# The first twelve attention steps of a fused attention + gated MLP kernel, written in another order: a split first group, two score tiles, and PE transposes for batch 0

## The chip, the cores and the metric

One core of a Trainium2 chip runs the whole kernel in one launch. The metric is device time in microseconds (us), the median of several executions. One execution was also profiled. PE is the matrix engine, DVE the vector engine, ACT the scalar engine (exponentials, logarithms, activations), POOL the general engine, and SP issues DMAs. PE writes to PSUM, a small memory of eight banks; a tile of 512 float32 per partition is one bank.

## The reference

Eight batches, twelve heads, 448 positions, head size 64. Attention with normalised q and k comes first, then a gated MLP over the concatenated heads.

```python
def rmsnorm(x, g):
    return x / np.sqrt(np.mean(x * x, axis=-1, keepdims=True) + 1e-06) * g
q_n, k_n = rmsnorm(q, g_q), rmsnorm(k, g_k)
attn = softmax(q_n @ k_n.T / np.sqrt(64))        # sums + 1e-9
x = (attn @ v) with the heads side by side       # (8, 448, 768)
h = np.maximum(x @ w_in, 0.0)                    # (8, 448, 1024)
u, v = h[..., :512], h[..., 512:]
v_n = (v - mean(v)) / np.sqrt(var(v) + 1e-06)
v_s = einsum('ts,bsd->btd', w_spatial, v_n) + b_spatial[None, :, None]
out = (u * v_s) @ w_out                          # (8, 448, 768) float32
```

## The kernel before

Positions are laid out 112 to a partition set, four chunks of them (NC). Four heads make a **group**, three groups a batch, so there are 24 groups, and four **steps** a group: step t computes scores and exponentials for two heads and two chunks of keys of group G = t // 4. There are 96 steps (0 to 95) and three more turns of the loop that only finish what is behind. Every engine takes its instructions strictly in the order in which the code is written (`manual_schedule`), so the order of the calls in the loop is the schedule.

**Preparing a group.** `load` brings q and k of a group (float32) on SP's queue into a ring of four tiles each (`qf`, `kf`). `squares` multiplies each by itself into `sqt` (POOL; ACT or DVE where `eng` says so), `reduce` sums them (DVE), `rstd` makes 1/rms on ACT (`lnms`, `rs`), and `scaled` multiplies the raw tile with it into bf16 (`n`). The products must then be transposed so that the head dimension lies on the partitions. Group 0 uses PE (`transposes`), and DVE brings the result from PSUM; every other group uses `transpose_dma`, a DMA on SP's queue (`qT`, `kr`), and `k_scale` multiplies k by the gains (`kT`) on DVE.

**A step.** `scores` writes four products of 448 columns into one tile `pss` of four PSUM banks, `expo` takes the exponential on ACT into `et`. In the first twelve steps each step goes in two halves of two banks, in the others in one piece. One group later `sums` and `recip` make the softmax denominators, and `values` (twice) and `xt_store` (DVE) the attention output `xt`. The other four PSUM banks (`ps_w`) rotate among everything else.

**The MLP** of batch b starts at step 12 b + 15: `unit_v`, `stats`, `ln_rstd`, `ln_apply`, `unit_u`, `unit_s`, `unit_o`, spread over twelve steps. `unit_v` and `unit_u` need `w_in`, which POOL's queue loads at step 1; `w_sp`, `w_out` and `bst` follow at step 4. At step 15 DVE copies `bst` into `w_spT`, and `w_sp_unit` transposes one quarter of `w_sp` in each of steps 15 to 18. The v tiles of a batch (`load_v`) and all weights are issued on POOL's queue, behind POOL's own arithmetic.

Of the kernel before, what the change touches and what calls it, by code (L numbers as in the profile page):

```python
# [18 lines left out]
def kernel(  # L19
# [34 lines left out]
    v_pool = ctx.enter_context(tc.tile_pool(name="vp", bufs=3))  # L54
# [3 lines left out]
    m_pool = ctx.enter_context(tc.tile_pool(name="mp", bufs=2))  # L58
    o_pool = ctx.enter_context(tc.tile_pool(name="op", bufs=4))
# [6 lines left out]
    def load(G, i, l0=0, nl=4):  # L66
        b, g = divmod(G, NG)
        if (G, i) not in raw:
            raw[G, i] = qk_pool.tile([P, 4, NC * D], FP, name="qf" if i == 0 else "kf")
        sync.dma_start(out=raw[G, i][:, l0:l0 + nl], in_=(q_g, k_g)[i][b][g][:, l0:l0 + nl])  # L70
# [30 lines left out]
    w_in = const.tile([128, 6, DF], BF)  # L101
# [73 lines left out]
    def qk_tiles(G):
        if G not in qkt:
            qkt[G] = (qt_pool.tile([128, NC, 2, P], BF, name="qT"),
                      qt_pool.tile([128, NC, 2, P], BF, name="kT"))
        return qkt[G]
# [374 lines left out]
```

## Time and profile before

| what | value |
| --- | --- |
| median of 3 runs | 356.57 us (354.12 to 356.83) |
| profiled execution, its own time | 354.63 us |
| its span from first to last instruction | 352.8 us |
| busy in the span: PE, ACT, DVE, POOL | 82%, 63%, 60%, 53% |

The profiled execution has its own time, 1.83 us more than its span; rows of the trace add up to the span. The busy shares are means over two different stretches: the first 80 us, in which PE is busy 33.39 us, and the rest. So the shares above bound nothing by themselves.

### The profile page before, as it was taken

Reading aid. Unit: us, or ns where it says so; the run is one execution under the profiler, and the core shown is the slowest. Engines: PE = TensorE matmul, PEld = TensorE weight load, DVE = VectorE, ACT = ScalarE, POOL = GpSimd, SP = SyncE. Lnnn points to the kernel's source line nnn. Section 1 sums busy time; section 2 is a strip of 40 time slices with the busy share of each in tenths; the row PEclk is TensorE's granted clock in tenths of the full one; section 3 lists DMA queues with packets and bytes.
Section 4 is the critical chain, followed back from the end, with each engine's and each line's share of the span. In section 5 each row is a group of like instructions: output and inputs, shape, how many; then the busy total and the mean of one; then the engine's idle time right before and its main releaser. Section 6 shows DMA issues by size and latency. Waiting matters only on the chain.

```text
span 352.8 us, 5856 instructions
## 1 busy us (share of the span) xinstructions
PE 288.7 (82%) x2338; PEld 134.5 (38%) x2338; DVE 210.6 (60%) x352; ACT 222.0 (63%) x273; POOL 186.3 (53%) x113
## 2 busy tenths in 40 slices
PE   0222634688999989997999989998999899999993
PEld 0111201224435433542344434443444345445552
DVE  3385304226887587757764886488648865745551
ACT  2334434375778768874876786778677867785331
POOL 7259850926746774687197549654965484000000
PEclk9999999999999999998999999999999999999998
DMA  7979999497346994899339983999299554302305
GB/s 194 245 159 167 203 187 203 89 148 156 55 110 144 209 243 106 145 213 248 101 82 215 242 170 69 220 252 166 58 223 261 62 54 111 99 2 62 96 0 158
DMA packets 81651, 52.26 MB, mean 148 GB/s; under 512 B 44271, under 2 KB 77264, under 8 KB 81624
## 3 DMA queue, kind: packets, MB, share of 16 engines
q1 hardware_dynamic: 69216, 43.59, 57.2%
q0 software_dynamic: 12400, 8.30, 16.6%
q8 instruction: 18, 0.29, 0.4%
q14 instruction: 9, 0.07, 0.1%
q10 hardware_dynamic: 8, 0.00, 0.0%
HBM read 38.58 MB, written 11.01 MB: 141 GB/s over the span
## 4 chain that ended last, share of the span: by engine, by line
issue 37%; POOL 34%; PE 18%; DMA 7%; ACT 1%; DVE 1%; ACTq 0%; POOLq 0%; DVEq 0%
POOL sqt L148 19%; POOL n L168 12%; PE ps L336 5%; DMA qT<-n 4%; PE ps L283 4%; PE ps L312 3%; PE pss L217 2%; PE ps L257 2%; PE ps L322 2%; POOL vt L74 2%; ACT et L228 1%; DMA out_dram<-osb 1%; DMA g_row<-in_g_k_dram 1%; PE ps L238 1%; POOL w_in L121 1%
## 5 line engine op out<-in xcount | busy, mean ns | idle before, releaser
L228 ACT ACTIVATE et<-pss 112x1792 bf16<-112x1792 f32 (+1 forms) x109 | 160.4, 1483 | 68.8 <-PE pss L217 67.9
L168 POOL TENSOR_TENSOR n<-qf,rs 112x1024 bf16<-112x1024 f32 (+1 forms) x25 | 48.5, 1939 | 111.3 <-ACT rs L163 109.4
L217 PE MATMUL pss<-qT,kT 64*112 64x448 bf16 x384 | 64.6, 408 | 39.9 <-ACT et L228 33.0
L155 DVE TENSOR_REDUCE ms<-sqt 112x16 f32<-112x1024 f32 (+1 forms) x50 | 58.1, 1171 | 40.4 <-POOL sqt L148 38.4
L265 DVE TENSOR_TENSOR xt<-ps,rc 128x448 bf16<-128x448 f32 x48 | 29.6, 617 | 41.2 <-PE ps L257 35.7
L217 PEld LDWEIGHTS <-kT 64*112 64x112 bf16 x384 | 22.1, 134 | 79.2 <-issue 66.8
L257 PE MATMUL ps<-et,vt 112*32 112x448 bf16 x768 | 49.6, 382 | 0.0
L336 PE MATMUL ps<-w_out,gt 128*112 128x384 bf16 x256 | 47.5, 330 | 1.7 <-DVE osb L341 1.4
L283 PE MATMUL ps<-w_in,xt 128*112 128x512 bf16 x192 | 45.8, 383 | 0.1
L148 POOL TENSOR_TENSOR sqt<-qf 112x1024 f32<-112x1024 f32 x23 | 44.4, 1932 | 0.0
L312 PE MATMUL ps<-xt,w_in 128*128 128x448 bf16 x192 | 41.3, 361 | 2.2 <-DVE vs L275 2.2
L168 POOL TENSOR_TENSOR n<-kf,rs 112x1024 bf16<-112x1024 f32 x21 | 40.0, 1906 | 0.0
L148 POOL TENSOR_TENSOR sqt<-kf 112x1024 f32<-112x1024 f32 x21 | 39.7, 1890 | 0.0
L336 PEld LDWEIGHTS <-gt 128*112 128x112 bf16 x256 | 31.3, 129 | 18.4 <-issue 11.1
L283 PEld LDWEIGHTS <-xt 128*112 128x112 bf16 x192 | 23.4, 130 | 19.4 <-issue 6.6
L341 DVE COPY osb<-ps 112x384 f32<-112x384 f32 x46 | 24.4, 553 | 7.5 <-PE ps L336 5.9
L322 PE MATMUL ps<-w_spT,vn 112*128 112x448 bf16 (+1 forms) x128 | 26.9, 353 | 0.0
L257 PEld LDWEIGHTS <-vt 112*32 112x32 bf16 x768 | 16.8, 100 | 26.4 <-issue 19.5
L312 PEld LDWEIGHTS <-w_in 128*128 128x128 bf16 x192 | 17.6, 100 | 24.2 <-issue 11.1
L238 PE MATMUL ps<-et,ones 112*32 112x448 bf16 x384 | 24.8, 382 | 0.0
L325 DVE TENSOR_TENSOR gt<-ps,us 128x448 bf16<-128x448 f32 x32 | 20.0, 625 | 6.8 <-PE ps L322 4.5
L289 DVE BATCH_NORM_STATS2 s<-vs 112x6 f32<-112x512 bf16 x32 | 21.8, 680 | 2.5 <-ACT vs L273 2.5
(47 smaller groups left out, 184.0 us busy)
## 6 DMA issues: line engine op xcount, KB each, us to landing
out_dram<-osb SPq DMA_DIRECT2D x31, 336.0 KB, 3.6
qf<-in_q_dram SPq DMA_DIRECT2D x23, 448.0 KB, 6.3
kf<-in_k_dram SPq DMA_DIRECT2D x23, 448.0 KB, 7.4
vt<-in_v_dram POOLq DMA_DIRECT2D x8, 672.0 KB, 13.0
w_in<-in_moe_w_in_dram POOLq DMA_DIRECT2D x4, 384.0 KB, 11.9
w_out<-in_moe_w_out_dram POOLq DMA_DIRECT2D x1, 768.0 KB, 13.7
qf<-in_q_dram SPq DMA_DIRECT2D x2, 224.0 KB, 3.6
kf<-in_k_dram SPq DMA_DIRECT2D x2, 224.0 KB, 3.8
```

The source lines that it names most:

```text
L148: (eng or pool).tensor_tensor(out=t[:, 0:nl, :], in0=x, in1=x, op=ALU.mult)
L155: dve.tensor_reduce(out=sqs[G][:, i, NC * l0:NC * (l0 + nl)], in_=sqt.pop((G, i, l0))[:, 0:nl, :].rearrange("p l (c d) -> p (l c) d", d=D) ...
L168: (eng or pool).tensor_tensor(out=nrm[G, i][:, :, l0:l0 + nl, :].rearrange("p c l d -> p l c d"), in0=raw[G, i][:, l0:l0 + nl, :].rearrang ...
L217: pe.matmul(out=pss[:, 2 * c + h, 0:S], lhsT=kT[64 * h:64 * h + 64, c0 + c, pr, :], rhs=qT[64 * h:64 * h + 64, :, pr, :], start=True, stop ...
L228: act.activation(out=exps[G, pr][:, 2 * c0 + a:2 * c0 + a + m, :], in_=pss[:, a:a + m, 0:S], func=AF.Exp, bias=0.0, scale=1.0)
L238: pe.matmul(out=ps[32 * l:32 * l + 32, 0:S], lhsT=ones, rhs=exps[G, l // 2][:, 2 * c + l % 2, :], start=(c == 0), stop=(c == NC - 1), tile ...
L257: pe.matmul(out=ps[32 * l:32 * l + 32, 0:S], lhsT=vb[b][:, 3 * l + g, c, 32 * half:32 * half + 32], rhs=exps[G, l // 2][:, 2 * c + l % 2, ...
L265: dve.tensor_tensor(out=xts[b][:, 2 * g + half, :], in0=pst.pop((G, half))[:, 0:S], in1=rec[G], op=ALU.mult)
L283: pe.matmul(out=ps[0:P, :], lhsT=xts[b][:, j, c * P:(c + 1) * P], rhs=w_in[:, j, DH:DF], start=(j == 0), stop=(j == 5))
L312: pe.matmul(out=ps[:, 0:S], lhsT=w_in[:, j, 128 * f:128 * f + 128], rhs=xts[b][:, j, :], start=(j == 0), stop=(j == 5))
L322: pe.matmul(out=ps[:, 0:S], lhsT=vn_t[b % 2][0:kp, c, 128 * f:128 * f + 128], rhs=w_spT[0:kp, c, :, :].rearrange("p c s -> p (c s)"), star ...
L336: pe.matmul(out=ps[0:P, 0:384], lhsT=gts[b][:, f, c * P:(c + 1) * P], rhs=w_out[:, f, r], start=(f == 0), stop=(f == 3))
```

## The change

The part of the program ahead of step 16 is written anew; the work from there on is the same, with smaller rings of buffers.

- Group 0 is split in two halves with tiles of their own (`first`), and ACT takes three of its four squares ahead of everything else. q and k of groups 0 to 4 are issued on SP before anything waits (`f`, `qf`, `kf`).
- For the first twelve steps, `pss` becomes two tiles `pse` of two banks each (`scores_half`, `expo_half`). At step 12 that pool is closed and `pss` takes its banks.
- Groups 1 to 4 are transposed on PE and brought from PSUM by DVE (`qe`, `ke`); `transpose_dma` starts with group 5. Of groups 1 to 4 the products `scaled` are shared by POOL and DVE.
- PE does 50 matmuls of 128 columns on the identity at the start, and eight in each of steps 0 to 3 (`dummies`); nothing reads them.
- `load_v(0)` moves behind the first work on POOL; `w_in` is two tensors loaded by four DMAs each, at steps 5 and 9; `w_sp` goes to step 9, `w_out` and `bst` to step 12.
- The rings `vp`, `mp` and `op` go from 3, 2 and 4 buffers to 2, 1 and 3. For later groups `k_scale` moves two steps later.

```diff
+    ps_e = early_pools.enter_context(tc.tile_pool(name="ps_e", bufs=2, space=PSUM, side="right"))
...
-    v_pool = ctx.enter_context(tc.tile_pool(name="vp", bufs=3))
+    v_pool = ctx.enter_context(tc.tile_pool(name="vp", bufs=2))
...
-    m_pool = ctx.enter_context(tc.tile_pool(name="mp", bufs=2))
-    o_pool = ctx.enter_context(tc.tile_pool(name="op", bufs=4))
+    m_pool = ctx.enter_context(tc.tile_pool(name="mp", bufs=1))
+    o_pool = ctx.enter_context(tc.tile_pool(name="op", bufs=3))
...
-    for G in (1, 2):
+    for G in (1, 2, 3):
         load(G, 0)
         load(G, 1)
...
+    def dummies(n):
+        for _ in range(n):
+            pe.matmul(out=ps_d[:, 0:128], lhsT=ident, rhs=ident, start=True, stop=True)
+
+    dummies(50)
...
     def transposes(G, pr):
...
-        qT, kT = qk_tiles(G)
-        dve.tensor_copy(out=qT[:, :, pr, :], in_=ps[:, 0:4, 0:P])
-        dve.tensor_scalar(out=kT[:, :, pr, :], in0=ps[:, 4:8, 0:P], scalar1=g2_col, scalar2=None,
-                          op0=ALU.mult)
+        qT = early_qt.tile([128, NC, P], BF, name=f"qe{pr}")
+        kT = early_qt.tile([128, NC, P], BF, name=f"ke{pr}")
+        dve.tensor_copy(out=qT, in_=ps[:, 0:4, 0:P])
+        dve.tensor_scalar(out=kT, in0=ps[:, 4:8, 0:P], scalar1=g2_col, scalar2=None, op0=ALU.mult)
+        qkt[G, pr] = (qT, kT)
...
+    def scores_half(t, c):
+        sct[t, c] = ps_e.tile([P, 2, 512], FP, name="pse")
+        scores_of(sct[t, c], t, c)
+
+    def expo_half(t, c):
+        expo_of(sct[t, c], t, 2 * c, 2)
...
+    squares(0, 0, 0, 2, act)
+    squares(0, 1, 0, 2, act)
+    squares(0, 0, 2, 2, act)
+    reduce(0, 0, 0, 2)
+    reduce(0, 1, 0, 2)
+    reduce(0, 0, 2, 2)
+    rstd(0, 0, 2)
+    squares(0, 1, 2, 2, act)
+    scaled(0, 0, 0, 2)
+    scaled(0, 1, 0, 2, dve)
...
+    squares(1, 0, eng=act)
+    squares(1, 1)
+    scores_half(0, 0)
+    scores_half(0, 1)
+    transposes(0, 1)
+    load_v(0)
+    squares(2, 0)
...
         if t == 0:
-            rstd(1)
-            scaled(1, 0)
-            scaled(1, 1, eng=dve)
-            squares(2, 0)
+            reduce(1, 0)
+            reduce(1, 1)
+            squares(2, 1)
         elif t == 1:
-            transpose_dma(1, 0)
-            transpose_dma(1, 1)
-            squares(2, 1, eng=dve)
+            rstd(1)
+            scaled(1, 1, eng=dve)
+            scaled(1, 0, eng=dve)
+        elif t == 4:
             reduce(2, 0)
             reduce(2, 1)
-        elif t == 2:
-            k_scale(1)
+        elif t == 5:
             rstd(2)
             scaled(2, 0)
-        elif t == 3:
             scaled(2, 1, eng=dve)
...
+            squares(3, 0)
+            squares(3, 1, eng=dve)
+            load_w_in(1)
...
+        elif t == 12:
+            reduce(4, 0)
+            reduce(4, 1)
+            load_w_out()
+        elif t == 13:
+            rstd(4)
+            scaled(4, 0)
+            scaled(4, 1, eng=dve)
...
+        if t < 4:
+            dummies(8)
...
+        if t == 15:
+            transposes(4, 0)
+            transposes(4, 1)
+        if t < 12:
+            turn = n == 3
+            if turn:
+                transposes(G + 1, 0)
+            if t + 1 < 12:
+                scores_half(t + 1, 0)
+            if turn:
+                transposes(G + 1, 1)
+            if t + 1 < 12:
+                scores_half(t + 1, 1)
+            if t == 7:
+                reduce(3, 0)
+                reduce(3, 1)
+            if t == 8:
+                rstd(3)
```

On POOL, these are the instructions from the product of group 2 (`n_264`) to the products of group 4 in the kernel before. `sqt` is a square, `n` a product with 1/rms, and DMA rows are issues.

```order
L168 TENSOR_TENSOR n_264<-qf,rs 112x4x4x64
L148 TENSOR_TENSOR sqt<-qf 112x1024
L148 TENSOR_TENSOR sqt<-kf 112x1024
L126 DMA w_sp<-in_moe_w_spatial_dram 112x1792
L127 DMA w_out<-in_moe_w_out_dram 128x4x768
L128 DMA bst<-in_moe_b_spatial_dram 17x448
L168 TENSOR_TENSOR n_331<-qf,rs 112x4x4x64
L168 TENSOR_TENSOR n_333<-kf,rs 112x4x4x64
```

On POOL in the changed kernel, this stands from the product of group 3 (`n_570`) to the squares of group 6.

```order
L189 TENSOR_TENSOR n_570<-qf,rs 112x4x4x64
L135 DMA w_in_u<-in_moe_w_in_dram 32x6x512 x4
L167 TENSOR_TENSOR sqt<-qf 112x1024
L80 DMA vt<-in_v_dram 112x12x256
L167 TENSOR_TENSOR sqt<-kf 112x1024
L140 DMA w_sp<-in_moe_w_spatial_dram 112x1792
L143 DMA w_out<-in_moe_w_out_dram 128x4x768
L144 DMA bst<-in_moe_b_spatial_dram 17x448
L189 TENSOR_TENSOR n_714<-qf,rs 112x4x4x64
L167 TENSOR_TENSOR sqt<-qf 112x1024
L167 TENSOR_TENSOR sqt<-kf 112x1024
```

The loads of weights and of the second v tile now stand between the work of groups 3 and 4, and the product of group 4 on POOL (`n_714`) has them all ahead of it.

On DVE, this stands around step 15 in the kernel before: the last `xt` of batch 0, a sum of squares, then the copies for `w_spT`, two relu (`vs`), and the k of group 4 (`kT`).

```order
L265 TENSOR_TENSOR xt<-ps,rc 128x448 x2
L155 TENSOR_REDUCE ms<-sqt 112x16
L471 CAST w_spT<-bst 17x448
L137 COPY w_spT<-ps 112x448
L275 TENSOR_SCALAR vs<-ps 112x512 x2
L155 TENSOR_REDUCE ms<-sqt 112x16
L205 TENSOR_SCALAR kT<-kr,g_col 128x896
```

And this in the changed kernel, from the product of group 4 (`n_716`) to the operands of group 4 (`qe_814`, `ke_815`).

```order
L189 TENSOR_TENSOR n_716<-kf,rs 112x4x4x64
L293 TENSOR_TENSOR xt<-ps,rc 128x448 x2
L173 TENSOR_REDUCE ms<-sqt 112x16 x3
L507 CAST w_spT<-bst 17x448
L153 COPY w_spT<-ps 112x448
L303 TENSOR_SCALAR vs<-ps 112x512 x2
L205 COPY qe_814<-ps 128x448
L206 TENSOR_SCALAR ke_815<-ps,g_col 128x448
```

Three sums (both of group 5, the first of group 6) and the copy of `bst` now stand ahead of the operands that step 16 needs.

## Rows read from the trace of the kernel before

**Rows 1.** Stretch, length, busy us of PE, PEld, DVE, ACT, POOL; PEclk; DMA.

```profile
50.00:60.00 10.00, 3.78 (x24) 1.37 (x25) 3.69 (x5) 3.10 (x5) 0.00 (x0) 1.00 1.28 211
...
90.00:100.00 10.00, 10.00 (x81) 4.31 (x79) 8.47 (x18) 7.91 (x12) 7.46 (x4) 1.00 0.51 102
```

**Rows 2.** Timeline to the first exponential: start us, us, engine, line, [idle before <-releaser].

```profile
7.19 0.31 ACT L162 ACTIVATE lnms<-ms,eps 112x16 f32<-112x16 f32 x1 [2.68 <-DVE ms L155]
...
9.43 0.93 PE L185 MATMUL ps<-ident,n 112*128 112x112 bf16 x8 [3.42 <-POOL n L168]
...
10.70 0.44 DVE L191 TENSOR_SCALAR kT<-ps,g_col 128x448 bf16<-128x448 bf16 x1
...
12.24 0.92 ACT L228 ACTIVATE et<-pss 112x896 bf16<-112x896 f32 x1 [4.49 <-PE pss L217]
```

**Rows 3.** Timeline of ACT: exponentials of steps 4 and 8, half of `recip`.

```profile
34.54 1.72 ACT L228 ACTIVATE et<-pss 112x896 bf16<-112x896 f32 x2 [1.08 <-PE pss L217]
...
39.18 0.58 ACT L247 ACTIVATE rc<-lr 128x448 f32<-128x448 f32 x1
...
55.11 1.72 ACT L228 ACTIVATE et<-pss 112x896 bf16<-112x896 f32 x2 [4.54 <-PE pss L217]
```

**Rows 4.** Timeline: DVE and POOL on groups 1 and 2.

```profile
23.03 1.23 DVE L168 TENSOR_TENSOR n<-kf,rs 112x1024 bf16<-112x1024 f32 x1 [0.65 <-ACT rs L163]
23.08 2.94 POOL L168 TENSOR_TENSOR n<-qf,rs 112x1024 bf16<-112x1024 f32 x1 [4.03 <-ACT rs L163]
24.18 2.92 DVE L148 TENSOR_TENSOR sqt<-kf 112x1024 f32<-112x1024 f32 x1
...
25.98 2.87 POOL L148 TENSOR_TENSOR sqt<-qf 112x1024 f32<-112x1024 f32 x1
```

**Rows 5.** Timeline: the transposing DMAs of group 3 and what waits.

```profile
45.47 7.04 SPq L197 DMA_TRANSPOSE qT<-n  x1
...
53.57 0.45 DVE L205 TENSOR_SCALAR kT<-kr,g_col 128x896 bf16<-128x896 bf16 x1 [9.17 <-DMA kr<-n]
53.94 0.62 DVE L265 TENSOR_TENSOR xt<-ps,rc 128x448 bf16<-128x448 f32 x1
```

**Rows 6.** Timeline of POOL: issues and a square.

```profile
28.80 0.99 POOL L74 DMA_DIRECT2D vt<-in_v_dram  x1
29.77 2.50 POOL L121 DMA_DIRECT2D w_in<-in_moe_w_in_dram  x4
...
34.83 1.88 POOL L148 TENSOR_TENSOR sqt<-qf 112x1024 f32<-112x1024 f32 x1
...
39.10 0.80 POOL L127 DMA_DIRECT2D w_out<-in_moe_w_out_dram  x1
```

**Rows 7.** An issue in the first 90 us: count, KB, us to landing.

```profile
bst<-in_moe_b_spatial_dram POOLq DMA_DIRECT2D x1, 29.8 KB, 13.1
```

**Rows 8.** Timeline around step 16: PE and DVE.

```profile
77.68 1.69 PE L257 MATMUL ps<-et,vt 112*32 112x448 bf16 x16
...
82.96 1.22 DVE L155 TENSOR_REDUCE ms<-sqt 112x16 f32<-112x1024 f32 x1 [2.92 <-POOL sqt L148]
...
83.50 0.59 PE L217 MATMUL pss<-qT,kT 64*112 64x448 bf16 x4
84.02 0.94 PE L238 MATMUL ps<-et,ones 112*32 112x448 bf16 x16
...
84.21 0.99 DVE L471 CAST w_spT<-bst 17x448 bf16<-17x448 f32 x1
...
85.54 1.28 DVE L275 TENSOR_SCALAR vs<-ps 112x512 bf16<-112x512 f32 x2
```

**Rows 9.** Timeline of SP and ACT: an output's first issue, a later copy.

```profile
109.84 0.35 SPq L345 DMA_DIRECT2D out_dram<-osb  x1
...
114.15 0.49 ACT L339 ACTIVATE osb<-ps 112x384 f32<-112x384 f32 x1
```

**Rows 10.** DMA issues of the page, whole span: KB each, us to landing.

```profile
out_dram<-osb SPq DMA_DIRECT2D x31, 336.0 KB, 3.6
```

More of the change, by code (lines that the diff above doesn't have):

```diff
@@ L67, in load @@
         b, g = divmod(G, NG)
[L68 to L70 removed]
+        if nl == 4:
+            t = qk_pool.tile([P, 4, NC * D], FP, name="qf" if i == 0 else "kf")
+        else:
+            t = first.tile([P, 2, NC * D], FP, name=f"f{i}{l0}")
+        raw[G, i, l0] = t
+        sync.dma_start(out=t, in_=(q_g, k_g)[i][b][g][:, l0:l0 + nl])
     def load_v(b):
@@ L98 @@
     make_identity(nc, ident)
-    w_in = const.tile([128, 6, DF], BF)
+    w_in_u = const.tile([128, 6, DH], BF)
+    w_in_v = const.tile([128, 6, DH], BF)
     w_out = const.tile([128, 4, DM], BF)
@@ L165, in scaled @@
+        rst[G, l0] = st_pool.tile([P, 2, 4 * nl], FP, name="rs")
+        act.activation(out=ln, in_=sqs[G, l0], func=AF.Ln, bias=eps[0:P, :], scale=1.0 / D)
+        act.activation(out=rst[G, l0], in_=ln, func=AF.Exp, bias=0.0, scale=-0.5)
     def scaled(G, i, l0=0, nl=4, eng=None):
-        if (G, i) not in nrm:
-            nrm[G, i] = qn_pool.tile([P, NC, 4, D], BF, name=f"n{i}")
+        if nl == 4:
+            t = qn_pool.tile([P, NC, nl, D], BF, name=f"n{i}")
+        else:
+            t = first.tile([P, NC, nl, D], BF, name=f"n{i}{l0}")
@@ L173, in scaled @@
             op=ALU.mult)
[L175 to L179, printed above, removed]
     def transposes(G, pr):
@@ L202 @@
-    krs = {}
+            krs[G] = t
+        else:
+            qts[G] = t
+    krs, qts = {}, {}
     def k_scale(G):
-        dve.tensor_scalar(out=qkt[G][1], in0=krs.pop(G), scalar1=g2_col, scalar2=None, op0=ALU.mult)
+        kT = qt_pool.tile([128, NC, 2, P], BF, name="kT")
+        dve.tensor_scalar(out=kT, in0=krs.pop(G), scalar1=g2_col, scalar2=None, op0=ALU.mult)
+        for pr in range(2):
+            qkt[G, pr] = (qts[G][:, :, pr, :], kT[:, :, pr, :])
     exps, xts = {}, {}
-    pss = ps_sc.tile([P, 4, 512], FP, name="pss")
@@ L232, with step @@
+    def step(t):
+        for c in range(2):
+            scores_of(pss[:, 2 * c:2 * c + 2, :], t, c)
+        expo_of(pss, t, 0, 4)
     rec, pst = {}, {}
@@ L349 @@
     NST = NGT * 4
-    for pr in range(2):
-        l = 2 * pr
-        squares(0, 0, l, 2, act)
-        squares(0, 1, l, 2, dve)
-        reduce(0, 0, l, 2)
-        reduce(0, 1, l, 2)
-        rstd(0, l, 2)
-        if pr == 0:
-            dve.tensor_copy(out=g2_col, in_=ps_g[:, 0:1])
-        scaled(0, 0, l, 2)
-        scaled(0, 1, l, 2, dve)
-        transposes(0, pr)
-        if pr == 0:
-            scores(0, 0)
-            scores(0, 1)
-            expo(0, 0)
-    squares(1, 0)
-    squares(1, 1, eng=dve)
@@ L445 @@
             transpose_dma(T, 1)
-        if n == 0 and 3 <= K < NGT:
-            k_scale(K)
         if moe:
```

169 lines of the change are left out of this document (85 added, 84 removed).

## The prediction

> **What bounds the kernel now.** I read the busy times by stretch first, then the time lines of the slow stretch. From 90 to 100 us PE is busy 10.00 of 10.00 us; from 50 to 60 it is busy 3.78, and POOL not at all [rows 1]. So the kernel is two things: a start in which everything waits for everything, and from step 16 on a PE that never stops. The four score products of step 16 start at 83.50 [rows 8]. The change leaves PE's work from there on as it is, so what it is worth is the time at which these four start. I call it X; before it is 83.50.
>
> What the start waits for is in the time lines. The first exponential is at 12.24 [rows 2], step 4 at 34.54 and step 8 at 55.11 [rows 3], about 5 us a step, while one step's exponentials take 1.72. Step 8 came late because SP held one transposing DMA for 7.04 us behind other traffic, and DVE, next in its queue, sat 9.17 us for the k of that DMA [rows 5].
>
> **The change, part by part.** I follow the new order with durations of before, each instruction behind the one ahead of it on its engine.
>
> *First exponential.* The chain from `rstd` (7.19) to the exponential (12.24) is the same work. ACT takes the k square as well, so `rstd` comes at about 6.8, and the transposes and scores take half their time if PE runs at its upper level (below). I put it at 11.1.
>
> *Group 0.* Eight halves of 0.92 [rows 2] follow with no wait for PE, since there are two tiles. In their middle ACT must do `rstd(1)`, which waits until DVE has done its evictions and two sums (1.22 each [rows 8]), at 15.1: half a us lost, and half a us of work. Group 0 ends at 19.4.
>
> *Group 1.* Both products are on DVE, and POOL squares group 2 beside them. What that costs is in the time line [rows 4]: a product that takes DVE 1.23 ran first, POOL's, begun beside it, took 2.94 and so ended one square's length (1.88 [rows 6]) after it, and DVE's next, a square of about 1.24 alone, took 2.92. Engine by engine they went one after the other. In the new order DVE starts at 15.8 behind a square begun at 14.5; 0.6 of wait, 1.23, 1.88 of POOL, 1.23 make 20.7. Without the mutual wait it would be 18.3. PE's transposes, two evictions of at most 0.44 [rows 2] and the scores (some 1.3 more) give step 4 at 22.9. The old 34.54 is thus 11.6 earlier.
>
> The Trainium skill ("SBUF — State Buffer", "SBUF: two separate sides") says that DVE with two SBUF inputs and a GpSimd instruction exclude each other for whole instructions; the trace agrees (2.94 and 2.92 [rows 4]). The page says the same lock keeps GpSimd from writing descriptors while DVE is in a two-port mode, which speaks against sharing; no row here shows it. As an estimate by that page, each of the two `w_in` issue blocks could lose one DVE instruction of 1.24, and the sum below would be some 1 us later.
>
> *PE's level.* Sixteen `values` products took 1.69 us at 77.68 and sixteen `sums` of equal size 0.94 at 84.02 [rows 8]; the granted clock reads 1.00 in the sparse and in the dense stretch alike [rows 1], so I take the two levels (1.2 and 2.4 GHz) from the durations. PE rose between the two, late and not at the start. At the low level a step costs PE 1.69 and four scores (twice 0.59 [rows 8]), 2.9, more than ACT; at the high level ACT's 1.72 rules. I keep both: group 1 takes 8.6 on ACT (4 x 1.72, two of 0.58 for `recip` [rows 3], some 0.55 for `rstd`, whose first half is 0.31 [rows 2]) or 11.4 on PE.
>
> The Trainium skill ("TensorE: Matmul & The Clock Gate", "HAM oscillation — how this bites in real kernels") says that PE drops to its lower rate when it waits long between bursts. That speaks against the dummies: they stand in steps 0 to 3, and the waits come at the turns of group behind them. By the page the late figure of each pair here would hold; if the dummies' level lasted, the early one. The pair ends 2.9 apart.
>
> *Group 2.* `rstd(2)` at 28.2 or 28.9; then on DVE and POOL in turn 1.23, 1.9, 1.24; DVE must also do two `xt` (0.62 each [rows 5]) before it evicts. Step 8 comes at 35.1 or 36.8, before at 55.11. Two halves, the second operands, `recip` and the sums of group 3 later, `rstd(3)` ends at 40.0 or 41.5.
>
> *The POOL queue.* From here POOL sets the time. It holds, in order: the product of group 3 behind DVE's (1.23 + 1.9), four issues of `w_in` (2.50), a square (1.88), the v issue (0.99), a square (1.88) [rows 6]: 10.4, at 50.4 or 51.9. The issues of `w_sp`, `w_out` and `bst` (at most 0.80 each [rows 6]) fit behind, beside the sum and `rstd(4)`, which ends at 52.3 or, as ACT is behind by then at the low level, 55.2. Then the product of group 4 (3.1 with DVE's ahead) and three squares (5.6): 61.0 or 63.9. On DVE a sum (1.22), the `bst` copy (0.99), a copy of an eviction's size (0.44 [rows 2]), two relu (1.28) and the evictions (0.83) stand between that and the scores of step 16 [rows 8, 2]: X = 65.8 or 68.7. No work hides this chain: PE and ACT have nothing else.
>
> *The weights.* `bst` is issued at 52.4 to 54 and took 13.1 to land before [rows 7]. Again that long, the copy on DVE would start at 65.5 to 67 instead of 62.2 to 65, so 3 us late. Those 13 us were in a queue full of `w_in` and transposes; the new queue holds `w_in`'s second half and a v tile. The cost is between 0 and 3; I take 1, nearer the low end because the transposes are gone. With the middle of the pair, 67.3, X = 68.3: 15.2 earlier.
>
> *Given back later.* Group 5 is the first with a transposing DMA, issued at step 16, and its `k_scale` stands at step 18 ahead of the statistics that ACT waits for; if it lands like an output (3.6 [rows 10]) DVE waits up to 3.7 and ACT up to 2, of which PE's queue hides most. I take 0.5. At the end the fourth output tile must wait for the first one's DMA since `op` has three: 0.4. `vp` and `mp` with fewer buffers cost nothing: v has 14 steps to land, and PE's order keeps a batch's MLP behind the last one's. If the cover of v went, it would hold PE for the rest of its landing.
>
> Sum: 354.63 (the profiled execution's own time, 1.94 below the median of 356.57) - 15.2 + 0.9 = 340.3. I predict 340.
>
> **Rivals.**
> 1. *Larger gain.* The mutual waits don't recur and PE stays at its upper level. Each of four pairs then gives back 1.2 to 2.4, 6.1 in all, from 65.8; X is then 59.7, or with `bst` landing after issue and 13 about 62. 354.63 - 21.5 + 0.9 = 334. For: ACT and PE have room. Against: the wait is there at each such pair [rows 4]. 0.2.
> 2. *About half.* Transfers come late: `w_sp`, which PE needs at step 15, and `bst`, or the DMA of group 5, a kind that held SP 7.04 us [rows 5]. From a landing of 70 on, each us counts: X = 74 and 346, or with 3 more for group 5's DMA 349. For: such landings were slow [rows 5, 7]. Against: four groups no longer use transposing DMAs. 0.17.
> 3. *Slower.* The output ring. Copies to the fourth tile are at 114.15, the first tile's DMA is issued at 109.84 [rows 9] and lands some 3.6 later [rows 10], so there was 0.7 of room. If that issue comes later behind SP's transposes, ACT waits at each batch with the exponentials behind it. It must cost more than 2.0 at each of seven batches to use up the 14.3, and 2.6 to be slower by over 1%: 358 or more at that. For: SP's order is strict. Against: ACT is idle a fifth of the time there [rows 1]. 0.03.
> 4. *Nothing.* The gain is given back, since POOL must from step 16 on make up for group 5 and each later group comes late as well: 353 to 358. POOL is busy 7.46 of 10 in the dense stretch [rows 1], so it catches up. 0.04.
>
> **How the numbers follow.** The forecast has 0.56, with 337 to 344 of its own (both levels, 0 to 3 for the weights, 0 to 2 for group 5). The range takes most of rivals 1 and 2: 332 to 347. About 1% (3.6 us) is what a measurement here can tell from no change. All but rivals 3 and 4 lie below 353: faster 0.93, same 0.04, slower 0.03.
>
> **What would show it.** In the changed profile: the first exponential at 11; step 4 at 23 and step 8 at 35 to 37, each behind a wait of ACT for PE that DVE ended; POOL without a gap from 40 to 51 and again to 61; the scores of step 16 at 66 to 70, freed by DVE's `ke`; DVE stopped by `bst` or POOL's squares at step 15; PE dense from there. I am wrong if step 8 is not before 42, if X is after 76, or if PE has new idle time after step 20.

## The result, and the profile after

| | before | after |
| --- | --- | --- |
| median | 355.35 us (353.88 to 356.83) | 338.85 us (337.58 to 339.43) |
| ratio | | 0.953 [0.947, 0.959] |
| profiled execution (its span) | 354.63 (352.8) | 337.58 (335.8) |

The kernel is faster by 16.5 us. The forecast was 340 with a range of 332 to 347. The scores of step 16, the X of the prediction, start at 68.54, forecast 68.3.

The first view of after is the busy time by stretch, with the columns of [rows 1].

```profile
10.00:20.00 10.00, 8.01 (x63) 4.72 (x59) 7.67 (x8) 8.21 (x12) 7.77 (x5) 0.66 1.13 241
...
50.00:60.00 10.00, 3.84 (x32) 1.27 (x24) 4.73 (x5) 5.08 (x5) 9.84 (x8) 0.56 1.27 209
60.00:70.00 10.00, 7.79 (x44) 4.26 (x48) 6.84 (x11) 0.42 (x1) 4.73 (x4) 0.67 0.99 170
70.00:80.00 10.00, 10.00 (x82) 4.55 (x71) 5.85 (x12) 6.28 (x9) 6.22 (x4) 0.74 0.39 85
...
90.00:100.00 10.00, 9.32 (x90) 4.66 (x88) 7.83 (x11) 6.94 (x7) 7.50 (x4) 1.00 0.40 89
```

From 50 to 60 PE is as idle as before (3.84 against 3.78 [rows 1]), but now POOL is full (9.84 against 0.00): its queue sets the time there. ACT does almost nothing from 60 to 70, and from 70 PE is nearly full (9.32 to 10.00 in the two lines shown). The start still is a stretch of waits; it is 15 us shorter.

The second view is the time line of after: start, length, engine, operation, and the idle time ahead with what ended it.

```profile
11.80 1.72 ACT L244 ACTIVATE et<-pse 112x896 bf16<-112x896 f32 x2 [0.33 <-PE pse L234]
15.36 1.91 POOL L167 TENSOR_TENSOR sqt<-qf 112x1024 f32<-112x1024 f32 x1
16.68 3.53 DVE L189 TENSOR_TENSOR n<-kf,rs 112x1024 bf16<-112x1024 f32 x1 [0.65 <-ACT rs L181]
17.21 1.90 POOL L167 TENSOR_TENSOR sqt<-kf 112x1024 f32<-112x1024 f32 x1
20.13 1.21 DVE L189 TENSOR_TENSOR n<-qf,rs 112x1024 bf16<-112x1024 f32 x1
23.84 0.92 ACT L244 ACTIVATE et<-pse 112x896 bf16<-112x896 f32 x1 [3.96 <-PE pse L234]
36.65 0.92 ACT L244 ACTIVATE et<-pse 112x896 bf16<-112x896 f32 x1 [3.32 <-PE pse L234]
41.45 2.94 POOL L189 TENSOR_TENSOR n<-qf,rs 112x1024 bf16<-112x1024 f32 x1 [3.26 <-ACT rs L181]
44.34 2.28 POOL L135 DMA_DIRECT2D w_in_u<-in_moe_w_in_dram  x4
49.46 1.91 POOL L167 TENSOR_TENSOR sqt<-kf 112x1024 f32<-112x1024 f32 x1
53.38 2.93 POOL L189 TENSOR_TENSOR n<-qf,rs 112x1024 bf16<-112x1024 f32 x1 [0.16 <-ACT rs L181]
59.98 1.88 POOL L167 TENSOR_TENSOR sqt<-qf 112x1024 f32<-112x1024 f32 x1
60.07 0.66 PE L149 MATMUL ps<-ident,w_sp 112*112 112x112 bf16 x4 [4.17 <-DMA w_sp<-in_moe_w_spatial_dram]
60.52 4.92 PE L311 MATMUL ps<-w_in_v,xt 128*112 128x512 bf16 x12
65.53 0.55 DVE L507 CAST w_spT<-bst 17x448 bf16<-17x448 f32 x1 [2.42 <-DMA bst<-in_moe_b_spatial_dram]
66.43 1.28 DVE L303 TENSOR_SCALAR vs<-ps 112x512 bf16<-112x512 f32 x2
68.03 0.45 DVE L206 TENSOR_SCALAR ke<-ps,g_col 128x448 bf16<-128x448 bf16 x1
68.54 0.99 PE L234 MATMUL pss<-qe,ke 64*112 64x448 bf16 x4 [1.42 <-DVE ke L206]
69.46 1.69 PE L266 MATMUL ps<-et,ones 112*32 112x448 bf16 x16
69.58 1.66 ACT L244 ACTIVATE et<-pss 112x1792 bf16<-112x1792 f32 x1 [11.98 <-PE pss L234]
```

Steps 4 and 8 come at 23.84 and 36.65 (34.54 and 55.11 [rows 3]), each behind a wait of ACT for PE. The k product of group 1 is the plainest sight of the mutual wait: alone it takes 1.23 [rows 4]; here, issued between two squares of POOL, it takes 3.53, so POOL's second square went ahead of it. POOL's queue is the chain from 41.45 on. At 61.86 it has done with the squares that DVE wants. Then DVE waits 2.42 for `bst`, takes it, evicts, and its `ke` frees the scores of step 16: the wait that ended last is the one for `bst`, and POOL's squares had about 2 us to spare. PE had waited 4.17 for `w_sp` too, but that lies beside the other wait. The third view, the DMA issues from 30 to 90 (KB, us to landing), has that transfer; it took 13.1 in [rows 7].

```profile
bst<-in_moe_b_spatial_dram POOLq DMA_DIRECT2D x1, 29.8 KB, 12.8
```

The starts of the exponentials of six steps, read from the time line of ACT, show where each kernel gains and loses (times in us; the last column is the median, and the ratio is to runs of the kernel before on the same chip):

| kernel | 4 | 8 | 13 | 16 | 20 | 95 | time, ratio |
| --- | --- | --- | --- | --- | --- | --- | --- |
| before | 34.5 | 55.1 | 75.0 | 84.1 | 97.6 | 320.5 | 355.35 |
| after | 23.8 | 36.7 | 49.7 | 69.6 | 84.6 | 303.5 | 338.85, 0.953 [0.947, 0.959] |
| e1 | 23.8 | 36.7 | 49.7 | 70.1 | 85.5 | 304.4 | 338.50, 0.952 [0.948, 0.958] |
| e2 | 23.0 | 35.3 | 49.6 | 67.1 | 81.5 | 300.4 | 335.64, 0.945 [0.939, 0.950] |
| e3 | 22.6 | 36.2 | 49.2 | 64.4 | 79.8 | 298.8 | 334.35, 0.943 [0.935, 0.952] |
| e4 | 23.7 | 37.3 | 51.7 | 61.4 | 82.2 | 301.9 | 334.66, 0.942 [0.937, 0.948] |
| e5 | 34.6 | 55.0 | 74.9 | 83.2 | 99.3 | 316.9 | 349.50, 0.982 [0.976, 0.987] |
| e6 | 23.4 | 37.0 | 51.4 | 68.6 | 84.6 | 303.7 | 338.09, 0.950 [0.944, 0.955] |
| e7 | 33.9 | 54.5 | 68.7 | 77.7 | 91.2 | 319.0 | 350.47, 0.984 [0.976, 0.991] |
| e8 | 24.7 | 37.4 | 51.2 | 68.6 | 85.6 | 306.8 | 339.46, 0.951 [0.943, 0.959] |
| e9 | 30.0 | 43.9 | 65.3 | 82.6 | 99.2 | 317.7 | 351.40, 0.983 [0.978, 0.988] |
| e10 | 21.6 | 36.6 | 51.0 | 69.2 | 84.8 | 303.3 | 337.24, 0.944 [0.940, 0.949] |
| e11 | 21.8 | 37.0 | 51.9 | 62.3 | 76.8 | 295.4 | 328.77, 0.919 [0.913, 0.925] |
| e12 | 22.8 | 37.4 | 50.8 | 59.9 | 74.8 | 293.4 | 326.87, 0.916 [0.910, 0.922] |

After against before: 25.4 us are won by step 13, 10.8 of them given back by step 16, 1.6 more by step 20 (12.95 are left), and 4.05 won back by step 95 (17.0).

Each row of steps is one profiled execution. e2, e3, e4 and e6 have the code of after up to step 4, and their step 4 comes between 22.6 and 23.8; e6 has it up to step 20, and its step 13 is at 51.4 for 49.7. So a difference of one or two us between two such rows shows nothing by itself.

### The profile page after: what moved, and what is told of

The parts are those of the page before. It is cut to its first block, busy times and chain, and to the rows that moved or that the text cites. A ratio compares the mean times of both kernels' runs of the same rounds, so it can differ in the third digit from the quotient of the medians.

```text
span 335.8 us, 6167 instructions
## 1 busy us (share of the span) xinstructions
PE 298.2 (89%) x2484; PEld 144.9 (43%) x2484; DVE 222.2 (66%) x364; ACT 223.5 (67%) x275; POOL 187.5 (56%) x114
## 4 chain that ended last, share of the span: by engine, by line
POOL 33%; issue 28%; PE 22%; DVE 6%; DMA 6%; ACT 3%; ACTq 0%; POOLq 0%; DVEq 0%; SPq 0%
POOL sqt L167 19%; POOL n L189 11%; PE ps L311 4%; DMA bst<-in_moe_b_spatial_dram 4%; PE ps L364 3%; PE ps L340 3%; PE ps L285 2%; PE pss L234 2%; PE ps L266 2%; ACT et L244 2%; PE ps L350 2%; POOL vt L80 2%; DVE n L189 1%; PE pse L234 1%; PE ps L200 1%
## 5 line engine op out<-in xcount | busy, mean ns | idle before, releaser
L244 ACT ACTIVATE et<-pss 112x1792 bf16<-112x1792 f32 x84 | 139.6, 1662 | 58.4 <-PE pss L234 57.5
L189 POOL TENSOR_TENSOR n<-qf,rs 112x1024 bf16<-112x1024 f32 x22 | 45.9, 2086 | 88.2 <-ACT rs L181 76.4
L173 DVE TENSOR_REDUCE ms<-sqt 112x16 f32<-112x1024 f32 x46 | 55.6, 1215 | 45.2 <-POOL sqt L167 45.2
L234 PE MATMUL pss<-qT,kT 64*112 64x448 bf16 x304 | 44.5, 369 | 5.8 <-ACT et L244 5.2
L311 PE MATMUL ps<-w_in_v,xt 128*112 128x512 bf16 x192 | 49.3, 404 | 0.0
L285 PE MATMUL ps<-et,vt 112*32 112x448 bf16 x768 | 46.1, 361 | 0.0
L340 PE MATMUL ps<-xt,w_in_u 128*128 128x448 bf16 x192 | 40.1, 354 | 0.0
L364 PEld LDWEIGHTS <-gt 128*112 128x112 bf16 x256 | 31.2, 129 | 19.9 <-issue 12.5
L234 PEld LDWEIGHTS <-kT 64*112 64x112 bf16 x304 | 14.9, 124 | 31.7 <-issue 31.4
L285 PEld LDWEIGHTS <-vt 112*32 112x32 bf16 x768 | 16.3, 97 | 25.4 <-issue 17.1
L244 ACT ACTIVATE et<-pse 112x896 bf16<-112x896 f32 x24 | 20.5, 913 | 9.6 <-PE pse L234 9.5
L340 PEld LDWEIGHTS <-w_in_u 128*128 128x128 bf16 x192 | 17.1, 98 | 20.9 <-issue 7.2
## 6 DMA issues: line engine op xcount, KB each, us to landing
vt<-in_v_dram POOLq DMA_DIRECT2D x8, 672.0 KB, 13.1
```

Source lines behind the costliest of these rows:

```text
L173: dve.tensor_reduce(out=sqs[G, l0][:, i, :], in_=sqt.pop((G, i, l0)).rearrange("p l (c d) -> p (l c) d", d=D), axis=AX.X, op=ALU.add)
L189: (eng or pool).tensor_tensor(out=t.rearrange("p c l d -> p l c d"), in0=raw[G, i, l0].rearrange("p l (c d) -> p l c d", d=D), in1=rst[G, ...
L234: pe.matmul(out=ps[:, h, 0:S], lhsT=kT[64 * h:64 * h + 64, 2 * (n % 2) + c, :], rhs=qT[64 * h:64 * h + 64, :, :], start=True, stop=True)
L244: act.activation(out=exps[G, n // 2][:, c0:c0 + m, :], in_=ps[:, 0:m, 0:S], func=AF.Exp, bias=0.0, scale=1.0)
L285: pe.matmul(out=ps[32 * l:32 * l + 32, 0:S], lhsT=vb[b][:, 3 * l + g, c, 32 * half:32 * half + 32], rhs=exps[G, l // 2][:, 2 * c + l % 2, ...
L311: pe.matmul(out=ps[0:P, :], lhsT=xts[b][:, j, c * P:(c + 1) * P], rhs=w_in_v[:, j, :], start=(j == 0), stop=(j == 5))
```

## The experiments

**e1: the idle matmuls left out.**

```diff
-    dummies(50)
...
-        if t < 4:
-            dummies(8)
```

> The changed kernel without the 50 + 32 matmuls on the identity. My theory (the start is set by DVE, POOL and ACT, and the level that the dummies buy is lost at the turns): first exponential 0.4 us later, since the first transposes take 0.93 again instead of 0.57; step 1 up to 1 us earlier, since eight dummies (1.06 us) no longer stand ahead of its scores; scores of step 16 within 0.7 us of 68.54; total within 0.7 us of the changed kernel. Rival (the dummies keep PE at its upper level through groups 0 and 1): sums and values of steps 4 to 7 at 1.69 instead of 0.94, step 8 about 2.9 us later, total 2 to 3 us more (some 341.5).

No difference: 338.50, and steps 4, 8 and 13 within 0.02 of where they were. In group 0 the dummies do speed PE up (the first eight transposes take 0.57 with them, 1.10 without), but the first exponential comes 0.36 earlier without them (11.44 for 11.80), not 0.4 later as expected. From step 4 on nothing of it is left: the sums at 25.14 take 1.69 in both kernels, and the `values` behind them 1.06 and 0.94, in after 0.94 and 0.94. So the dummies are not what brings PE to its upper level there, and no gain from them can be seen.

**e2: the bias row and `w_sp` issued at step 5. e3: group 4's transposes first at step 15. e4: both.**

```diff
# e2: load_bst() and load_w_sp() moved on POOL's queue
         elif t == 5:
...
+            load_bst()
+            load_w_sp()
             load_w_in(1)
# e3: PE's and DVE's order at step 15
         elif t == 15:
+            transposes(4, 0)
+            transposes(4, 1)
             reduce(5, 0)
...
-        if t == 15:
-            transposes(4, 0)
-            transposes(4, 1)
```

> The changed kernel with the issues of bst and w_sp moved from steps 12 and 9 to step 5, ahead of the first half of w_in, where POOL has time (it idles 38.2 to 41.4). Theory (step 16 waits for the order of POOL's and DVE's queues and, on top, for bst): the copy of bst follows the last sum at 63.1 instead of 65.5, PE needs not wait for w_sp from 55.9 to 60.07, and step 16's scores start at 66.2 to 67 instead of 68.54: 1.5 to 2.4 us less, 336.5 to 337.4. Rival (what lands by step 16 is a matter of bytes, whatever the order): w_in or the second v tile come later by as much, scores of step 16 at 68.5 and the total unchanged.

> The changed kernel with group 4's transposes and their evictions moved to the front of step 15 on PE and DVE, ahead of the two sums of group 5 and the copy of bst, and the sum of group 6 moved behind the relus. Theory: the operands of step 16 are ready at 59 instead of 68.5, but PE does w_sp's transposes (which wait for w_sp until 60.07) and twelve unit_v products (4.92 us) ahead of its scores, so these start at 65.4: 3 us less, about 336. Rival (bst alone holds DVE and so everything): scores of step 16 stay at 68.5 or the wait moves to step 17, total within 1 us of the changed kernel.

> Both edits together: bst and w_sp at step 5, group 4's transposes at the front of step 15. Theory: PE goes from step 15's scores (end 55.9) through transposes, w_sp and unit_v without a wait, scores of step 16 at 62.5 to 63.5: 5 to 6 us less, 333 to 334. Rival (bytes): no better than the better one of the two alone, 336. If group 5, whose products come behind POOL's squares, is the next wait, step 20 shows it: then the gain at step 20 is smaller than at step 16.

The time lines of e2, e3 and e4, in that order:

```profile
61.65 2.00 DVE L510 CAST w_spT<-bst 17x448 bf16<-17x448 f32 x1
...
66.10 1.00 PE L236 MATMUL pss<-qe,ke 64*112 64x448 bf16 x4 [1.07 <-DVE ke L208]
```

```profile
59.44 0.66 PE L149 MATMUL ps<-ident,w_sp 112*112 112x112 bf16 x4 [1.85 <-DMA w_sp<-in_moe_w_spatial_dram]
...
63.78 0.59 PE L234 MATMUL pss<-qe,ke 64*112 64x448 bf16 x4
...
64.99 0.56 DVE L510 CAST w_spT<-bst 17x448 bf16<-17x448 f32 x1 [4.17 <-DMA bst<-in_moe_b_spatial_dram]
```

```profile
72.02 4.67 DVE L224 TENSOR_SCALAR kT<-kr,g_col 128x896 bf16<-128x896 bf16 x1 [1.27 <-DMA kr<-n]
...
78.33 0.30 ACT L327 ACTIVATE lv<-mv,eps 112x4 f32<-112x4 f32 x1 [6.68 <-DVE mv L320]
```

With the weights early (e2) DVE no longer waits for `bst`, and the scores of step 16 start at 66.10, 2.4 earlier. Not all of that need be the edit's, because steps 4 and 8 of e2, ahead of what it changes, are 0.8 and 1.4 earlier too. From the end of the last sum ahead of the cast of `bst` to the scores it is 4.48 (5.42 in after); the wait is gone, but the cast takes 2.00 for 0.55. So the weights cost between 0.9 and 2.4 at step 16; the median gained 3.2. With the transposes first (e3) the scores start at 63.78 although DVE now waits 4.17 for `bst`: that wait has no scores behind it any more. So the order, in which the scores stand behind three sums, the bias row, a copy and two evictions of `vs`, cost more than the weights. Both together (e4) bring them to 60.81, 7.7 earlier and earlier than expected, and gain nothing over e3, where 333 to 334 was expected: `k_scale` of group 5, 0.45 where nothing is in its way [rows 5], takes 4.67 while three instructions of POOL end one after the other, the statistics and ACT come 6.68 late, and by step 20 e4 is behind e3.

This stall, which the prediction put at 0.5, is in every version that transposes group 5 by DMA. ACT's wait for these statistics, 0.75 in the kernel before, is 1.18 in after, 1.22 in e2, 2.20 in e3, about 3.0 in e1, e6, e9 and e10, 5.31 in e8 and 6.68 in e4; in e11 and e12, where PE transposes group 5, it is 0.75 again.

**e5 and e6: the place of `k_scale`.** In e5 the kernel before gets the later place, in e6 the changed one the earlier place back.

```diff
# e5, on the kernel before
-        if n == 0 and 3 <= K < NGT:
+        if n == 2 and 3 <= K < NGT:
# e6, on the changed kernel
-        if n == 2 and 5 <= K < NGT:
+        if n == 2 and K == 5 or n == 0 and 6 <= K < NGT:
```

> The kernel before, with the scaling of a group's transposed k moved from the first step ahead of the group to the third, as the changed kernel has it; nothing else. Between step 20 and step 95 the changed kernel is 4 us shorter than the kernel before (step 95 is 17.0 us earlier, step 20 only 12.95). Theory: that comes from this move. Then step 20 stays at 97.6 and step 95 comes at about 316.5 (before 320.46), with step 43 at about 166 (before 168.84), and the time is 351 to 353. Rival: it comes from something else (tiles per pair, the split w_in, fewer buffers): the time stays at 355 to 356 and step 95 at 320.

> The changed kernel, with the scaling of k put back to the first step ahead of the group for groups 6 on. Theory that the move is worth the 4 us: step 20 stays at 84.6, step 95 comes at 306 to 307.5 instead of 303.46, time 341 to 343. Rival, that other edits are: 338 to 339.5, step 95 at 303.5.

The time line of the kernel before has one long stall behind step 20:

```profile
161.16 1.84 DVE L205 TENSOR_SCALAR kT<-kr,g_col 128x896 bf16<-128x896 bf16 x1 [2.36 <-DMA kr<-n]
...
164.45 1.34 PE L312 MATMUL ps<-xt,w_in 128*128 128x448 bf16 x6 [2.22 <-DVE vs L275]
...
167.98 0.30 ACT L297 ACTIVATE lv<-mv,eps 112x4 f32<-112x4 f32 x1 [4.92 <-DVE mv L290]
```

DVE waits for the transposed k, PE for DVE's eviction of `vs` behind it. In e5 that stall is gone, steps 31 to 43 take 34.98 instead of 38.17, and the kernel before gains 1.8% (1.3 to 2.4). Step 95 is where it was expected (316.9); step 20 is 1.7 late, and 349.50 is below the 351 to 353 expected. The profiled execution gained 3.5 (351.14 for 354.63). In e6 the same edit backwards costs nothing: k is waited for again, about once a batch, here the longest time,

```profile
194.46 0.45 DVE L222 TENSOR_SCALAR kT<-kr,g_col 128x896 bf16<-128x896 bf16 x1 [2.54 <-DMA kr<-n]
```

but steps 43 to 91 take 139.56 against 139.40. So the theory holds for the kernel before and falls for the changed one: some other edit had taken the long stall out already. Which one (the later v loads, the rings, the split `w_in`) was not tried.

**e7 and e8: the score tiles alone.** e7 gives the kernel before the two tiles and nothing else; e8 takes them from the changed kernel.

```diff
# e7, on the kernel before
+            if half is not None:
+                sct[t, c] = ps_e.tile([P, 2, 512], FP, name="pse")
+            ps = pss[:, 2 * c:2 * c + 2, :] if half is None else sct[t, c]
...
# e8, on the changed kernel
+    one = ps_e.tile([P, 4, 512], FP, name="pse")
...
-        sct[t, c] = ps_e.tile([P, 2, 512], FP, name="pse")
+        sct[t, c] = one[:, 2 * c:2 * c + 2, :]
```

> The kernel before, with two score tiles of two banks for the first twelve steps in place of one of four, and nothing else of the change. Theory: the start waits above all for the preparation of the groups. Then step 4 comes at 30 to 34 (before 34.54) and step 8 no earlier than 52 (before 55.11, behind group 2's transposing DMA), the steps inside a group shrink from 5 to about 3 us, and the scores of step 16 come 1 to 6 us before 83.5; time 350 to 355. Rival, that the tiles carry most of the 15 us: step 4 at 26, step 8 at 40, time 340 to 346.

> The changed kernel with one score tile of four banks, its halves used in turn, for the first twelve steps, so that scores wait for the whole tile again; all else as changed. Theory (preparation carries most): steps inside groups 0 to 2 take 4 to 5 us instead of 2.5 to 3, step 4 comes at 26 to 30 (23.84), step 8 at 42 to 46 (36.65), the scores of step 16 at 72 to 78 (68.54), time 342 to 348. Rival, that the tiles carry most: scores of step 16 after 80, time above 350. Second rival, that the POOL queue of steps 9 to 14 hides it: 339 to 341.

In e7, DVE's `k_scale` of group 2 and the scores behind it:

```profile
53.30 0.45 DVE L206 TENSOR_SCALAR kT<-kr,g_col 128x896 bf16<-128x896 bf16 x1 [11.20 <-DMA kr<-n]
...
53.81 0.99 PE L221 MATMUL pse<-qT,kT 64*112 64x448 bf16 x4 [9.86 <-DVE kT L206]
```

The steps inside a group shrink, the waits for k grow instead (DVE's from 9.17 to 11.20), and step 8 stays at 54.5. Only from there on do the tiles win 6.4 us at step 16. They are not kept: by step 95 only 1.5 are left (319.0 for 320.5). The long stall of ACT (4.92), which the profiled execution of the kernel before has once, at 167.98, comes three times here; these are the first and the last:

```profile
126.11 0.30 ACT L302 ACTIVATE lv<-mv,eps 112x4 f32<-112x4 f32 x1 [4.92 <-DVE mv L295]
...
202.44 0.30 ACT L302 ACTIVATE lv<-mv,eps 112x4 f32<-112x4 f32 x1 [4.92 <-DVE mv L295]
```

So most of what e7 wins at step 16 does not reach the end of this execution; the median of e7 is 1.6% lower (0.9 to 2.4). In e8 the loss of the tiles shows in steps 4 and 8 by under 1 us and at step 16 not at all, and 339.46 is what the second rival expected. Its profiled execution (341.0) loses 3.3 behind step 17, where the tiles are no longer in use and DVE waits 4.00 for the k of group 5; two of its four executions (337.8 and 337.9) are as fast as after. So at step 16 the tiles are worth 6.4 us in the old order and nothing that can be seen in the new one. A likely reason, not tried by itself: in the old order a step's second scores are issued at its start and its successor's first ones at its end, both on one tile, while in the new one the two halves are issued together.

**e9: the transposing DMAs given back to groups 1 to 4.**

```diff
             scaled(1, 0, eng=dve)
+            transpose_dma(1, 0)
+            transpose_dma(1, 1)
...
             if turn:
-                transposes(G + 1, 0)
+                k_scale(G + 1)
```

> The changed kernel with the transposes of groups 1 to 4 given back to transposing DMAs and one scaling of k per group, at the places where the products and the evictions stand now; all else as changed. Theory: early transposing DMAs land late, as group 2's k did in the kernel before (issued at 36.28, landed at about 53.5). Then step 4 comes at 28 to 32 (23.84), step 8 at 45 to 53 (36.65), the scores of step 16 at 76 to 84 (68.54), time 346 to 354. Rival: such a DMA lands within some 3 us of its issue as group 5's does, step 4 at 26, step 8 at 40, and the POOL queue and the landing of the bias row hide the rest: scores of step 16 at 69 to 71, time 338 to 341.

The time line of e9, DVE's `k_scale` of groups 1 and 3, and the scores of step 16:

```profile
28.80 0.45 DVE L222 TENSOR_SCALAR kT<-kr,g_col 128x896 bf16<-128x896 bf16 x1 [8.13 <-DMA kr<-n]
...
61.03 0.45 DVE L222 TENSOR_SCALAR kT<-kr,g_col 128x896 bf16<-128x896 bf16 x1 [9.82 <-DMA kr<-n]
...
81.54 0.99 PE L234 MATMUL pss<-qT,kT 64*112 64x448 bf16 x4 [7.73 <-DVE kT L222]
```

Three waits for k, 8.13, 2.38 and 9.82, and the scores of step 16 at 81.54: of the 15.0 us that the change wins there, 13.0 are gone when this one part is left out. 351.40 is 12.6 over the changed kernel. That is what the PE transposes carry beside all the other parts; alone, on the kernel before, they were not tried, and e7 and e8 show that the worths of the parts do not add up.

**e10: group 1's products shared by POOL and DVE.**

```diff
-            scaled(1, 0, eng=dve)
+            scaled(1, 0)
+            squares(2, 0)
+            squares(2, 1)
```

> The changed kernel with group 1's q product on POOL, ahead of the two squares of group 2, and its k product on DVE as before. Theory (one engine at a time while both inputs are in SBUF): the two products end together at about 19.5 instead of 21.3, step 4 comes at 22 to 22.5 (23.84) and step 8 at 35 to 35.5 (36.65), the scores of step 16 0 to 1.5 earlier; time 337 to 339. Rival: the squares of group 2, now 3 us later, hold group 2: step 4 earlier, step 8 at 36.7 or later, no gain.

Step 4 comes 2.2 earlier, step 8 at the same 36.6: `values` of step 5 now wait 4.33 for v, issued at 13.89 and only then landed. The squares of group 2 that the rival named stand later too, and the run does not tell the two apart. The 1.6 us of the median (its range is 336.6 to 338.2) are hardly beyond the scatter.

**e11 and e12: a version that takes the next waits as well.**

```diff
# e11: e4, e10's edit, and
-            squares(3, 1, eng=dve)
+            squares(3, 1)
...
-            load_w_in(0)
             squares(4, 0)
-            load_v(1)
             squares(4, 1)
+            load_w_in(0)
+            load_v(1)
...
+        if t == 19:
+            transposes(5, 0)
+            transposes(5, 1)
# e12: further
+    load_v(0)
     squares(1, 1)
...
-            elif n < 3:
+            elif n - (G == 1) in (1, 2):
...
+        elif t == 8:
+            rstd(3)
```

> The order of e4 (transposes of group 4 first at step 15, bias row and w_sp issued at step 5) with what its trace showed late next: group 1's product as in e10, both squares of group 3 on POOL, the squares of group 4 ahead of the second half of w_in and of v, the statistics of groups 2 and 4 on ACT a step earlier, and group 5 transposed by PE and not by DMA. Theory (the chain over POOL sets the start): step 8 at 32 to 34 (e4: 37.31), the scores of step 16 at 54 to 57 (e4: 60.81), no wait for k at step 18, step 20 at 70 to 74 (82.2), time 325 to 329. Rival: something else holds each step, in the first place a late w_in or w_sp: scores of step 16 at 59 to 61 and time 330 to 334. Second rival: the gain at step 16 is given back by step 20 again: time 334 to 336.

> The order of e11 with the waits that its trace showed next: the first v issued ahead of the square of group 1's k (in e11 it landed at about 29.8 and held PE 4.4), the values of group 0 one step later, the sums of group 3's squares around group 2's evictions and group 3's statistics right behind step 8's exponentials. Theory (each us of the chain over POOL before step 16 is one us of the whole): step 8 at 34 to 35 (e11: 37.00), POOL's product of group 3 at 36.5 to 38 (41.26), the scores of step 16 at 57 to 59 (61.69), time 324 to 327. Rival: the landing of the first half of w_in, of w_sp or of group 5's data holds step 15 or 16, scores of step 16 at 61 or later: 328 to 330.

The time lines of e11 and of e12:

```profile
29.87 1.68 PE L287 MATMUL ps<-et,vt 112*32 112x448 bf16 x16 [4.37 <-DMA vt<-in_v_dram]
...
61.69 0.59 PE L236 MATMUL pss<-qe,ke 64*112 64x448 bf16 x4
```

```profile
59.26 0.59 PE L236 MATMUL pss<-qe,ke 64*112 64x448 bf16 x4
```

e11 hits the time (328.77) by another way than its theory: step 8 is at 37.0, not 32 to 34, and the scores of step 16 are at 61.69, no earlier than in e4; v held step 5 as in e10. What it wins over e4 is the stall of group 5, gone with its DMA: step 20 at 76.8 against 82.2. e12 also comes to its time (326.87, 12 us under the changed kernel) and misses its early steps: v holds PE only 0.50 now, yet step 8 stays at 37.4, and POOL's product of group 3 starts at 40.93, not at 36.5 to 38. PE, at its low level, has two `values` of 1.69 ahead of the second half of group 2's transposes; that these hold step 8 was not tried. The scores of step 16 come 2.4 earlier than in e11.

## Why the prediction was right, step by step

- **What it is worth is X.** X came out right: the change wins 15.0 there (forecast 15.2). That was in part luck. POOL's squares ended 0.6 ahead of the middle of their pair, and the work of DVE behind them took 1.9 more with the wait for `bst`, where 1 was put. And X is not the whole: e7 wins 6.4 at step 16 and keeps 1.5. PE also does stop behind X. Between X and step 95 it is idle 11.6 us in the kernel before and 8.4 in the changed one.
- **Given back later.** 0.5 was put for group 5. But 2.0 of the gain were lost from X to step 20, and here the forecast's term was too small. In after, PE is at its low level there: the four scores, sixteen sums and six `unit_v` products of step 16 take 0.99, 1.69 and 2.76, where PE at its upper level takes 0.59, 0.94 [rows 8] and 1.46 (the next one, at 76.48), and step 17 follows step 16 by 5.69, before by 4.16. That alone is not the cause. e6 has the same code up to step 20, and its scores of step 16 ran at the upper level, but its step 20 is at the same 84.60:

```profile
68.02 0.59 PE L234 MATMUL pss<-qe,ke 64*112 64x448 bf16 x4 [1.43 <-DVE ke L206]
...
77.61 2.08 DVE L222 TENSOR_SCALAR kT<-kr,g_col 128x896 bf16<-128x896 bf16 x1 [0.79 <-DMA kr<-n]
...
81.35 0.30 ACT L325 ACTIVATE lv<-mv,eps 112x4 f32<-112x4 f32 x1 [3.03 <-DVE mv L318]
```

  There the k of group 5 and ACT's wait behind it use up what PE's level gives. The ring of three output tiles, put at 0.4, shows its wait once, at the end, and costs under 0.1: the eight last copies start within 4.61 from first to last, before within 4.55.

```profile
329.83 0.49 ACT L367 ACTIVATE osb<-ps 112x384 f32<-112x384 f32 x1 [1.00 <-DMA out_dram<-osb]
```

  And 4.05 were won later, three of them the stall at 161, which the prediction did not have. So 354.63 - 15.2 + 0.9 should have read 354.63 - 15.0 + 2.0 - 4.1 = 337.5. The two missing sizes went in opposite directions, so the nearness of 340 to the measured time is luck as well.
- **The early steps.** The first exponential, the end of group 0, step 4, step 8 and the end of `rstd(3)` were forecast at 11.1, 19.4, 22.9, 35.1 or 36.8, and 40.0 or 41.5; they came at 11.8, 19.9, 23.8, 36.7 and 41.4. The late figure of each pair held, but step 4 was 0.9 late already: from step 4 to step 8 it took 12.8, between the two forecasts (12.2 and 13.9). PE was at either level here: the sums at 25.14 and 37.94 took 1.69, the `values` at 27.55 and 43.36 took 0.94. The Trainium skill ("TensorE: Matmul & The Clock Gate", "HAM oscillation — how this bites in real kernels") says that PE falls back to its lower rate when it waits long between bursts; the granted clock of after agrees (0.66 from 10 to 20, 0.56 from 50 to 60, 1.00 from 90 to 100).
- **One engine at a time.** The term was 0.6 of wait and 1.88 of POOL between DVE's two products; in the trace POOL's second square went in before DVE's first (3.53), with about the same sum: 21.3 for 20.7.
- **POOL's queue** held to within the pair: forecast end of the squares 61.0 or 63.9, measured 61.86. That it sets the time up to there was right, but not that it does so alone: DVE then waited for `bst`, and e3 and e4 take 4.8 and 7.7 us off X without a change to POOL's arithmetic. The 4.8 us of DVE's work that the prediction put behind the last square took 6.6 with the wait for `bst`, and, as e3 shows, most of it need not stand ahead of the scores.
- **The weights** were taken at 1 of 0 to 3. `bst` landed after 12.8 us again and DVE stood 2.42: the upper end. The transposes' absence did not make it faster. In e2, where that wait is gone, X is 2.4 earlier, at least 0.9 of it by the edit. The four issues of each half of `w_in` took 2.29 and 2.28 (2.50 [rows 6]), so the 1 us that DVE's instructions might have cost there shows nowhere.
- **The transposing DMAs.** The prediction read in [rows 5] that a DMA of 7.04 held step 8. That row is group 3's q. The k for which DVE waited was group 2's, one row earlier in the time line of the kernel before:

```profile
36.28 8.10 SPq L197 DMA_TRANSPOSE kr<-n  x1
```

  It was issued at 36.28, held SP's queue 8.10, and DVE went on at 53.57. The cause was the right one, the row was not. e9 shows what hangs on it: without the PE transposes 13 of the 15 us are gone, and the tiles, the sharing and the new order, all that is left in e9, win 2.0 at X. The prediction never split its gain between these parts.
- **The rivals.** The larger gain failed as its condition did: the mutual waits recurred (3.53, 2.94). The output ring (slower) has the one wait of 1.00 above and none in the batches before. "About half" was the weights and group 5: DVE's wait for the first was 2.42, ACT's behind the second 1.18 in after and up to 6.68 in e4; neither came near half of the gain.

## What to carry to other kernels

Ask of each wait in a starting phase what is late next before pricing its removal: here tiles, sharing and early weights are each worth nothing or a few us alone, because the next wait, often a transfer, holds the same step, and the edits of e12 together bring 12 us more than the change. A transposing DMA in the traffic of the first loads took 3 to 17 us to bring its k, so small transposes that gate the first steps belong on PE. An instruction that waits in an in-order queue is cheap only if nothing urgent stands behind it: the late bias row held the scores while it stood ahead of their operands (a wait of 2.42), and behind them a longer wait (4.17 in e3) did not. And an earlier start is worth only what the later steps keep: 6.4 us at step 16 became 1.5 at step 95 in e7.

## What the runs showed of the hardware

- POOL can go twice in a row while DVE waits: a product of 1.23 with both inputs in SBUF took 3.53, and a `k_scale` of 0.45, from SBUF to SBUF, took 4.67 in e4 while three instructions of POOL ended. The Trainium skill ("SBUF — State Buffer", "SBUF: two separate sides") has the exclusion of DVE and GpSimd for whole instructions; these two durations fit it, with a price of more than one instruction. No run isolates it.
- The granted clock of the records and the durations need not say the same. In after the column (behind POOL's) reads 0.56 to 0.74 in the stretches where sixteen products take 1.69; in e1 it reads 1.00 from 20 to 30, where the sums of 25.14 take the same 1.69; and in the kernel before, by stretch as in [rows 1], it reads 1.00 around the product of 1.69 at 77.68 [rows 8]:

```profile
70.00:80.00 10.00, 8.33 (x64) 2.92 (x63) 3.33 (x5) 7.66 (x10) 3.65 (x4) 1.00 0.85 150
```

- A transfer of 29.8 KB took 12.8 us when issued behind `w_sp` and `w_out` (392 and 768 KB) on POOL's queue, and 4.3 us ahead of them (e2). It was also issued 18 us earlier there; whether the queue or the traffic of that time made it slow was not told apart.
